# Query transposes moved to the DMA engines, with queries projected first, keys transposed in halves and token values kept in DRAM

## The chip, the cores and the metric

The kernel runs on one core of one Trainium2 chip. The metric is the device time of one execution in microseconds (us). The kernel before takes 1243.91 us in the median of the three runs that were at hand when the prediction was made (1236.84 to 1247.9). A time below is the median of all runs of a kernel, with their range. All runs quoted here gave the right result.

## The reference, cut to what matters

The work is one transformer block: a recurrent attention over 64 segments of 32 tokens with eight memory rows, then a gated feed-forward part.

```python
mem = mem0                                        # 8 rows of 640
for s in range(n_seg):                            # 64 segments, one after the other
    xs = x[:, s * seg_len:(s + 1) * seg_len, :]   # 32 tokens, layer-normed
    h = jnp.concatenate([mem, xs], axis=1)        # 40 rows
    q = jnp.einsum('btd,dhe->bhte', h, Wq)        # 32 heads of 128; k and v likewise
    scores = jnp.einsum('bhqe,bhke->bhqk', q, k) * scale
    p = softmax(where(mask, scores, -1e9))
    o = jnp.einsum('bhqk,bhke->bhqe', p, v)
    o = jnp.einsum('bhte,hed->btd', o, Wo)
    mem = o[:, :M, :]                             # the next segment's memory
    outs.append(o[:, M:, :])
...                                               # then h + FFN(layernorm(h))
```

The memory makes the loop a recurrence: the projections of segment s+1 can't begin before the memory rows of segment s have gone through the scores, the value product and the output projection. Whatever is late on that path is paid 62 times.

## The kernel before

Each segment projects a tile of 32 rows: the eight memory rows, and with them 24 token rows ("riders") of later segments. Four segments make a block. The 32 tokens of a block that find no place as riders ("extras") are projected separately, their keys at the end of a segment of position 2 (segment number mod 4), their queries in position 3, their values in position 0. Token keys wait in a ring `Kr`, token queries in `Qr`, token values in a ring `Vr`. `KS` holds the transposed keys of the current tile, `Vp` its values.

A projection leaves two [128, 512] tiles (four head groups of 32 rows each) in PSUM. They are copied to SBUF (`tok`) and have to be transposed before they can enter the scores. Keys are transposed by DMA (`dma_t`), queries by TensorE (`trans8`). In the loop all DMAs are issued from one queue, SyncE's, in program order; a DMA whose input isn't ready holds up all behind it (in the changed kernel 47 loads of values hold it for up to 6.4 us each). The segment's body:

```python
project(a, ks, 1, (0,), (P2,));  to_tok(P2, 0, "act")      # keys first
project(a, ks, 1, (1,), (P3,));  to_tok(P3, 1, "dve")
dma_t(KS..., tokp[0][:, :], ..., [("KS",)])                # one transpose, 128 x 1024
if fin: fin()                                              # extras' queries: trans8
pv_x(s - 1, BQ[0]);  norm_x(BQ[0]);  trans_ox(s - 1)       # token value product of s-1
project(a, ks, 0, (0, 1), (P0, P1))                        # queries
to_tok(P0, 2, "act");  to_tok(P1, 3, "dve")
project(a, ks, 2, (0,), BQ[:1])                            # values, first half
trans8(tok[2], ..., tok[3], ..., P3)                       # query transposes on TensorE
...                                                        # copies to Qr, Kr
project(a, ks, 2, (1,), (T0,))                             # values, second half
scores(s);  exp_mem();  exp_x()
v_riders(par, t0, nr)                                      # Vp -> Vr, 4 or 8 small DMAs
pv_mem(s);  trans_om(s);  wo_pass(...)                     # memory path
to_act(s + 1, B(T1), bank(T1)[:, 0:160])                   # new memory rows, on VectorE
store_attn(...)                                            # 4 DMAs
if evac: evac()                                            # extras' token tiles, Kr transpose
if woe: woe_sum(BQ[0]);  woe_store(s // 4 - 1)             # 8 DMAs, end of position 1
```

Token values go from the tile to the ring within SBUF:

```python
for g in range(4):
    a = 32 * g + M + done
    dma(Vr[q][32 * g + o:32 * g + o + m, :, :], Vp[par][a:a + m, :, :], ...)
```

The softmax here doesn't subtract the row's maximum and nothing guards it: scores larger than these inputs give would overflow.

Of the kernel before, what the change touches and what calls it, by code (L numbers as in the profile page):

```python
# [163 lines left out]
def build_kernel(nc, A_x, A_mem0, A_Wq, A_Wk, A_Wv, A_Wo, A_seg_len, B_W_gate, B_W_up, B_W_down, out):  # L164
# [21 lines left out]
    xn2_d = nc.dram_tensor("xn2_d", [128, DC, TB], BF16)  # L186
    attn_d = nc.dram_tensor("attn_d", [S, 4, DC * 32], BF16)
# [34 lines left out]
    mca = ar.alloc("mca", [128, SEG], BF16)  # L222
# [4 lines left out]
    KS = ar.alloc("KS", [128, H, SEG], BF16)  # L227
    Kr = [ar.alloc(f"Kr{i}", [128, H, SEG], BF16) for i in range(RING // SEG)]
    Qr = ar.alloc("Qr", [128, H, RING // SEG, M + SEG], BF16)
    Vr = [ar.alloc(f"Vr{i}", [128, 8, VW], BF16) for i in range(RING // SEG)]  # L230
# [50 lines left out]
    for g in range(4):  # L281
        add("pool", lambda p, g=g: p.affine_select(mca[32 * g:32 * g + 32, :], mca[32 * g:32 * g + 32, :], [[1, SEG]],
                                                   ALU.is_ge, 0.0, base=0, channel_multiplier=-1),
            r=[("mca",)], w=[("mca",)])
    add("dve", lambda v: v.memset(mbd[:], 0.0), w=[("mbd",)])
    for g in range(4):
        add("dve", lambda v, g=g: v.memset(mbd[32 * g:32 * g + 32, 0, 8 * g:8 * g + 8], BIG), r=[("mbd",)], w=[("mbd",)])
        add("dve", lambda v, g=g: v.memset(mbd[32 * g:32 * g + M, 1, 8 * g:8 * g + 8], BIG), r=[("mbd",)], w=[("mbd",)])

    add("dve", lambda v: v.memset(bank(P1), 0.0), w=[B(P1)])  # L290
# [5 lines left out]
    for i in range(RING // SEG):  # L296
        add("pool", lambda p, i=i: p.memset(ap(Vr[i], Dh, [[VW, 8], [1, 1]]), 1.0), w=[("Vr1", i)])
# [95 lines left out]
    def evac_k(src, skey, t0, n, lo, eng):  # L393
        for q, o, m, lo in pieces(t0, n, lo):
            copy_op(eng, Kr[q][:, :, o:o + m], src[:, :, lo:lo + m], [skey], [("Kr", q)])

    def evac_q(b, t0, n, lo, eng):
        for q, o, m, lo in pieces(t0, n, lo):
            copy_op(eng, Qr[:, :, q, M + o:M + o + m], slots(b, lo, lo + m), [B(b)], [("Qr", q)])
# [4 lines left out]
    def v_riders(par, t0, n):  # L404

        done = 0
        while done < n:
            t = t0 + done
            q, o = seg_slot(t // SEG), t % SEG
            m = min(n - done, SEG - o)  # L410
            for g in range(4):
                a = 32 * g + M + done
                dma(Vr[q][32 * g + o:32 * g + o + m, :, :], Vp[par][a:a + m, :, :], r=[("Vp", par), ("Vp1", par), ("Vr1", q)],
                    w=[("Vr", q, g, o)])
            done += m

    def vr_keys(q):
        return [("Vr", q)] + [("Vr1", q)] + [("Vr", q, g, o) for g in range(4) for o in (0, 8, 16, 24)]
# [11 lines left out]
    def ln1_back(b, src, r, eng):  # L430
# [13 lines left out]
        for j in range(full):  # L444
            copy(act_r[b % 2][:, j, :, M:32], src[:, :, RID * j:RID * (j + 1)], [("act", b % 2, "x", j)])
        if n == 128:
            copy(act_e[b % 2][:, :, :], src[:, :, 96:128], [("acte", b % 2)])
        elif n % RID:
            copy(act_r[b % 2][:, full, :, M:M + n % RID], src[:, :, RID * full:n], [("act", b % 2, "x", full)])
# [12 lines left out]
    def to_act(s, wkey, src):  # L462

        b, j = s // 4, s % 4
        add("dve", lambda v: v.transpose(TBf[:].rearrange("p c t -> p (c t)"), src), r=[wkey], w=[("TBf",)])  # L465
        add("dve", lambda v: v.tensor_copy(act_r[b % 2][:, j, :, 0:M], TBf[:, :, 0:M]), r=[("TBf",)],  # L466
            w=[("act", b % 2, j, "m")])
# [3 lines left out]
    def scores(s):  # L471

        q = seg_slot(s)

        def f(pe):
            for k in range(8):
                for a in range(2):
                    for g in range(4):
                        h = 4 * k + g
                        if a == 0:  # L480
                            o, lh = bank(P0)[32 * g:32 * g + 32, 40 * k:40 * k + 40], Kr[q][:, h, :]
                        else:
                            o, lh = bank(P1)[32 * g:32 * g + M, 40 * k:40 * k + 40], KS[:, h, 0:M]
                        i = pe.matmul(o, lh, Qr[:, h, q, :], start=True, stop=True, skip_group_check=True)  # L484
            return i
        add("pe", f, r=[("KS",), ("Qm", q), ("Kr", q), ("Qr", q)], w=[B(P0), B(P1)])

# [13 lines left out]
    def exp_x():  # L501
        add("act", lambda a: a.activation(Px[:, :].rearrange("p (a k q) -> p a k q", a=2, k=8), s_view(M, M + SEG),
                                          ACTF.Exp, scale=SCALE), r=[B(P0), B(P1)], w=[("Px",)])
        add("dve", lambda v: v.tensor_tensor(ap(Px, 0, [[32, 8], [1, 32]]), ap(Px, 0, [[32, 8], [1, 32]]),
                                             ap(mca, 0, [[0, 8], [1, 32]]), ALU.min), r=[("Px",), ("mca",)],
            w=[("Px",)])

    def pv_mem(s):
        q = seg_slot(s)
        par = s % 2  # L510
        for a in range(2):
            def f(pe, a=a):
                t = Vr[q] if a == 0 else Vp[par]
# [6 lines left out]
            add("pe", f, r=[("Pbd", a)] + ([("Vp", par), ("Vp1", par)] if a else vr_keys(q)), w=[B(T1)])  # L520
# [5 lines left out]
    def trans_om(s):  # L526
# [5 lines left out]
        copy_op("dve", ap(oT[s % 2], 0, [[16 * SEG, 2], [SEG, 4], [4 * SEG, 4], [1, M]]),  # L532
# [29 lines left out]
    def store_attn(src, skey, p0, t0, n):  # L562
        for g in range(4):
            dma(attn_d[t0:t0 + n, g, :], src[32 * g + p0:32 * g + p0 + n, :, :].rearrange("p c j -> p (c j)"),
                r=[skey], w=[("attn", t0, g)])

    def pv_x(s, b0):
        q = seg_slot(s)
        par = s % 2

        def f(pe):
            for kh in range(2):
                for a in range(2):
                    for c in range(4):
                        k = 4 * kh + c
                        for g in range(4):
                            n, t = (32, Vr[q]) if a == 0 else (M, Vp[par])
                            i = pe.matmul(bank(b0 + g)[32 * c:32 * c + 32, 129 * kh:129 * kh + 129],  # L578
                                          Px[32 * g:32 * g + n, 256 * a + 32 * k:256 * a + 32 * k + 32],
                                          t[32 * g:32 * g + n, k, 0:129], start=(a == 0), stop=(a == 1),  # L580
                                          skip_group_check=True, tile_position=(32 * g, 32 * c))
            return i
        add("pe", f, r=[("Px",), ("Vp", par), ("Vp1", par)] + vr_keys(q), w=[B(b0 + g) for g in range(4)])
# [15 lines left out]
    def copy_oTe(s):  # L599
        o = M * (s % 4)  # L600
        copy_op("dve", oTe[:, :, o:o + M], oT[s % 2][:, :, 0:M], [("oT", s % 2, "m")], [("oTe", s % 4)])


    def attn_keys(i):
        ks = []
        for s in range(4 * i, 4 * i + 4):
            ks += [("attn", 32 * s + M, g) for g in range(4)] + [("attn", 32 * s, g) for g in range(2)]
        return ks
# [29 lines left out]
    for g in range(4):  # L638
        dma(wtok[1][32 * g:32 * g + M, :, :],
# [27 lines left out]
    def opening_back(j, n, bk):  # L667
        t = 2 * (n % 2)
        trans8(tok[t], ("tok", t), tok[t + 1], ("tok", t + 1), bk)
        if n > 0:  # L670
            eng = ("dve", "act")[n - 1]
            if j == 1:
                evac_k(slots(bk, 0, SEG), B(bk), 32 * (n - 1), 32, 0, eng)
            else:
                evac_q(bk, 32 * (n - 1), 32, 0, eng)
            return
        q = seg_slot(0)
        if j == 1:
            copy_op("dve", KS[:, :, 0:M], slots(bk, 0, M), [B(bk)], [("KS",)])
            evac_k(slots(bk, 0, SEG), B(bk), 64, RID, M, "act")  # L680
        else:
            copy_op("dve", Qr[:, :, q, 0:M], slots(bk, 0, M), [B(bk)], [("Qm", q)])
            evac_q(bk, 64, RID, M, "act")
# [19 lines left out]
    for i in range(2):  # L703
        for n, (a, ks) in enumerate(groups):
            q = seg_slot(n - 1)
            t, key = (Vr[q], ("Vr", q)) if n else (Vp[0], ("Vp", 0))
            project(a, ks, 2, (i,), vbanks[n][i:i + 1])
            to_v(vbanks[n][i], t, i, key, ("act", "dve")[(i + n) % 2])
    v_riders(0, 64, RID)
# [15 lines left out]
    def extra_units(s):  # L725
# [15 lines left out]
        def evac():  # L741
            for i, e in enumerate(("act", "dve")):
                if j == 2:
                    to_v(BQ[i], Vr[q], i, ("Vr", q), e)
                else:
                    to_tok(BQ[i], 2 + i, e)
            if j == 1:
                dma_t(Kr[q][:].rearrange("p h t -> p (h t)").rearrange("p (k r) -> p k r", r=128), tokp[1][:, :],
                      [("tok", 2), ("tok", 3)], [("Kr", q)])

        def fin():
            trans8(tok[2], ("tok", 2), tok[3], ("tok", 3), P2)
            evac_q(P2, t0, 32, 0, "act")
        return part, evac, (fin if j == 0 else None)
# [10 lines left out]
    def woe_store(b):  # L765
        for j in range(4):
            for dg in range(2):
                t0 = 32 * (4 * b + j)
                dma(attn_d[t0:t0 + M, 2 * dg:2 * dg + 2, :].rearrange("t g f -> t (g f)"),
                    ap(Pbd, 0, [[1, 320]], 32 * dg + M * j, M), r=[("Pbd", 0), ("Pbd", 1)], w=[("attn", t0, dg)])  # L770

    fin = None
    for s in range(NSEG):
# [13 lines left out]
        if s > 0:  # L787
            a, ks = pass_act(s)
            t0, nr = rider_tokens(s)
            project(a, ks, 1, (0,), (P2,))  # L790
            to_tok(P2, 0, "act")
            project(a, ks, 1, (1,), (P3,))
            to_tok(P3, 1, "dve")
            dma_t(KS[:].rearrange("p h t -> p (h t)").rearrange("p (k r) -> p k r", r=128), tokp[0][:, :],
                  [("tok", 0), ("tok", 1)], [("KS",)])
            if fin:
                fin()
            pv_x(s - 1, BQ[0])
            norm_x(BQ[0])
            trans_ox(s - 1)  # L800
            n = n_rows(nb) if s % 4 == 2 and ln else 128 if e2b is not None else 0
            if n:
                row_scale(xt, ("xt",), n, xt, ("xt",))
                dma_t(chunks_of(at[:, :])[:, :, 0:n], xt[0:n, :], [("xt",)], [("at",)])
# [6 lines left out]
            project(a, ks, 2, (0,), BQ[:1])  # L811
            to_v(BQ[0], Vp[par], 0, ("Vp", par), "act")
            if not last:
                trans8(tok[2], ("tok", 2), tok[3], ("tok", 3), P3)
# [226 lines left out]
```

## Time and profile before

| | before |
|---|---|
| time | 1243.91 us (1236.84 to 1247.9, 3 runs) |
| span of the profiled run, granted TensorE clock | 1245.2 us, 0.983 |
| opening / 62 segments / feed-forward tail | 62.2 / 971.7 / 211.3 us |
| segment mean, positions 0 / 1 / 2 / 3 | 15.65 / 14.83 / 16.48 / 15.60 us |
| half-clock time within the loop | 24.4 us, 7 stretches |

The rows from the third on are my sums over the trace. Position 2 is given without the next-to-last segment of the loop, which also loads weights (with it 16.61). A segment runs from the VectorE transpose of one segment's memory rows (`TBf`) to the next one's.

From the page of the kernel before: busy time, the clock in tenths over 40 slices, and the engines' shares of the chain of work that ended last. A group's columns are: line, engine and operation, output and inputs, count, then busy us and mean ns, then the idle time ahead of it and what ended most of it.

```profile
PE 1114.9 (90%) x30140; PEld 577.0 (46%) x27792; DVE 564.4 (45%) x1438; ACT 333.2 (27%) x684; POOL 25.3 (2%) x92
...
PEclk9889999999999999999999999999999998999999
...
PE 77%; DMA 11%; DVE 6%; SPq 3%; issue 3%; ACT 1%; DVEq 0%
...
L350 PE MATMUL ps<-W,act_r 128*32 128x512 bf16 x6640 | 456.5, 385 | 27.7 <-DVE act_r L466 12.7
...
L369 PE MATMUL ps<-ident,tok 128*128 128x128 bf16 x664 | 51.2, 220 | 17.9 <-DVE tok L378 13.3
...
L484 PE MATMUL ps<-Qr,Kr 128*32 128x40 bf16 x2048 | 41.9, 186 | 25.2 <-DMA KS<-tok 25.0
```

TensorE sets the time: it is busy for 90% of the span and makes up 77% of the chain. The query transposes (L369) cost it 51.2 us and 17.9 us of waiting. The scores (L484) wait 25.0 us in all for the transposed keys.

Four successive segments, that one first (window, its length, then busy us of PE, PEld, DVE, ACT and POOL with counts, granted clock, DMA share, GB/s):

```profile
657.75:674.34 16.59, 14.05 (x450) 7.40 (x402) 7.05 (x19) 4.16 (x8) 0.00 (x0) 1.00 0.53 87
674.34:690.44 16.10, 14.38 (x458) 7.59 (x410) 8.92 (x24) 5.57 (x11) 0.00 (x0) 1.00 0.40 86
690.44:705.80 15.36, 14.00 (x466) 8.20 (x442) 7.20 (x19) 4.22 (x9) 0.00 (x0) 1.00 0.28 55
705.80:721.24 15.44, 14.14 (x456) 7.20 (x407) 8.33 (x23) 4.66 (x11) 1.48 (x5) 1.00 0.36 68
```

TensorE is busy for 14.0 to 14.4 us of each, at full clock.

### The profile page before, as it was taken

What the parts mean: (1) busy time and instruction counts of PE and PEld (TensorE: products, weight loads), DVE (VectorE), ACT (ScalarE), POOL (GpSimd) and SP (SyncE); (2) the same over time, 40 slices, a digit from 0 to 9 for tenths busy, and PEclk for the clock granted to TensorE, in tenths of its full rate; (3) what the DMA queues carried; (4) which work ended last, traced back from release to release, by engine and by line L of the source; (5) the groups of instructions that cost most, each with busy time, mean ns of one, the idle gap of its engine ahead of it and who ended that gap; (6) DMA issues with size and microseconds to landing.
All of it is one profiled execution on the core that took longest, in us unless ns stands there. A gap on an engine that the chain in (4) does not pass through costs nothing.

```text
span 1245.2 us, 62156 instructions
## 1 busy us (share of the span) xinstructions
PE 1114.9 (90%) x30140; PEld 577.0 (46%) x27792; DVE 564.4 (45%) x1438; ACT 333.2 (27%) x684; POOL 25.3 (2%) x92
## 2 busy tenths in 40 slices
PE   5589999989899989989988989999989986999998
PEld 2344445444445544544444544454445454533443
DVE  3244545444444444554544544454445442443522
ACT  2123223322232222232322222233223321211311
POOL 1000000000000000000000000000000000000000
PEclk9889999999999999999999999999999998999999
DMA  9933333324343334343434344423242329121200
GB/s 360 337 53 68 58 67 59 66 57 67 56 66 59 70 57 66 60 81 66 79 70 81 66 82 64 65 55 79 42 78 57 63 58 323 27 80 27 69 22 22
DMA packets 218274, 102.12 MB, mean 82 GB/s; under 512 B 190688, under 2 KB 206752, under 8 KB 218016
## 3 DMA queue, kind: packets, MB, share of 16 engines
q1 hardware_dynamic: 217824, 98.13, 36.8%
q8 instruction: 227, 3.72, 1.3%
q14 instruction: 31, 0.25, 0.1%
q10 hardware_dynamic: 192, 0.01, 0.0%
HBM read 36.79 MB, written 6.55 MB: 35 GB/s over the span
## 4 chain that ended last, share of the span: by engine, by line
PE 77%; DMA 11%; DVE 6%; SPq 3%; issue 3%; ACT 1%; DVEq 0%
PE ps L350 27%; PE ps L541 13%; PE ps L336 10%; PE ps L883 10%; DMA KS<-tok 5%; DMA Kr<-tok 3%; SPq L306 3%; PE ps L484 3%; PE ps L369 3%; PE ps L916 3%; PE ps L578 3%; PE ps L553 2%; DMA Wo<-in_A_Wo_dram 2%; PE ps L517 2%; DVE TBf L465 2%
## 5 line engine op out<-in xcount | busy, mean ns | idle before, releaser
L350 PE MATMUL ps<-W,act_r 128*32 128x512 bf16 x6640 | 456.5, 385 | 27.7 <-DVE act_r L466 12.7
L350 PEld LDWEIGHTS ps<-W,act_r 128*32 128x32 bf16 x6640 | 170.0, 97 | 275.4 <-issue 74.3
L541 PE MATMUL ps<-Wo,oT 128*32 128x160 bf16 x8448 | 165.3, 236 | 35.2 <-DVE oT L378 23.8
L378 DVE CAST tok<-ps 128x512 bf16<-128x512 f32 x161 | 111.1, 690 | 151.6 <-PE ps L350 97.3
L541 PEld LDWEIGHTS ps<-Wo,oT 128*32 128x32 bf16 x8448 | 149.1, 98 | 49.5 <-DVE oT L378 35.5
L376 ACT ACTIVATE tok<-ps 128x512 bf16<-128x512 f32 x161 | 95.9, 596 | 249.9 <-PE ps L336 134.6
L336 PE MATMUL ps<-W,act_r 128*32 128x512 bf16 x1240 | 120.6, 379 | 0.3 <-issue 0.3
L376 ACT ACTIVATE wtok<-ps 128x160 bf16<-128x160 f32 x64 | 19.5, 304 | 311.4 <-DVE TBf L465 302.3
L465 DVE STREAM_TRANSPOSE TBf<-ps 128x160 f32<-128x160 f32 x64 | 22.4, 350 | 174.6 <-PE ps L541 174.6
L350 PE MATMUL ps<-W,act_e 128*32 128x512 bf16 x900 | 94.2, 395 | 1.5 <-issue 1.5
L336 PE MATMUL ps<-W,act_e 128*32 128x512 bf16 x900 | 93.3, 392 | 0.8 <-issue 0.8
L591 DVE TENSOR_TENSOR ox<-ps,rx 128x512 bf16<-128x512 f32 x128 | 82.5, 686 | 2.2
L376 ACT ACTIVATE Qr<-ps 128x768 bf16<-128x768 bf16 (+3 forms) x110 | 69.2, 658 | 42.0 <-DVE Qr L378 26.7
L369 PE MATMUL ps<-ident,tok 128*128 128x128 bf16 x664 | 51.2, 220 | 17.9 <-DVE tok L378 13.3
L883 PE MATMUL ps<-xn2T,Wg 128*128 128x512 bf16 x260 | 65.6, 383 | 0.0
L883 PE MATMUL ps<-xn2T,Wu 128*128 128x512 bf16 x260 | 65.5, 383 | 0.0
L484 PE MATMUL ps<-Qr,Kr 128*32 128x40 bf16 x2048 | 41.9, 186 | 25.2 <-DMA KS<-tok 25.0
L898 DVE TENSOR_TENSOR hT<-g,ps 128x512 bf16<-128x512 bf16 (+1 forms) x56 | 38.5, 688 | 57.1 <-PE ps L883 53.3
L916 PE MATMUL ps<-Wd,hT 128*128 128x320 bf16 (+1 forms) x240 | 63.3, 300 | 0.0
L369 PEld LDWEIGHTS ps<-ident,tok 128*128 128x128 bf16 x664 | 37.4, 98 | 52.8 <-DVE tok L378 48.0
L378 DVE CAST Vp<-ps 128x512 bf16<-128x512 f32 x64 | 44.1, 689 | 33.1 <-PE ps L350 33.1
L896 ACT ACTIVATE g<-ps 128x512 bf16<-128x512 f32 (+1 forms) x56 | 32.5, 593 | 95.9 <-PE ps L883 95.9
(82 smaller groups left out, 1006.1 us busy)
## 6 DMA issues: line engine op xcount, KB each, us to landing
Vr<-Vp SPq DMA_DIRECT2D x124, 48.8 KB
W<-in_A_Wk_dram SPq DMA_DIRECT2D x2, 2560.0 KB
W<-in_A_Wq_dram SPq DMA_DIRECT2D x2, 2560.0 KB
W<-in_A_Wv_dram SPq DMA_DIRECT2D x2, 2560.0 KB
Wo<-in_A_Wo_dram SPq DMA_DIRECT2D x2, 2560.0 KB
xt<-in_A_x_dram SPq DMA_DIRECT2D x30, 160.0 KB
Vr<-Vp SPq DMA_DIRECT2D x128, 32.5 KB
attn_d<-wtok SPq DMA_DIRECT2D x256, 7.5 KB
```

What stands on the lines that cost most here:

```text
L336: return pe.add_instruction(mybir.InstMatmult(name=nc.get_next_instruction_name(), engine=mybir.EngineType.PE, ins=[pe.lower_ap(rhs), pe.l ...
L350: ins = pe.matmul(*a, start=(c == 0), stop=(c == DC - 1), skip_group_check=True)
L369: ins = pe.matmul(bank_bf(b)[:, k * 128:(k + 1) * 128], t[:, (k % 4) * 128:(k % 4 + 1) * 128], ident[:, :], is_transpose=True)
L376: add("act", lambda a: a.activation(dst, src, ACTF.Copy), r=r, w=w)
L378: add("dve", lambda v: v.tensor_copy(dst, src), r=r, w=w)
L465: add("dve", lambda v: v.transpose(TBf[:].rearrange("p c t -> p (c t)"), src), r=[wkey], w=[("TBf",)])
L484: i = pe.matmul(o, lh, Qr[:, h, q, :], start=True, stop=True, skip_group_check=True)
L541: i = pe.matmul(bank(bk)[32 * gg:32 * gg + 32, 0:160], src[:, hb, :], w[:, gg], start=(hb == 0), stop=(hb == 31), skip_group_check=True)
L591: add("dve", lambda v, kh=kh: v.tensor_tensor(ox[:, kh, :, :], src[:, :, kh, 0:128], ap(rx, kh, [[2, 4], [0, 128]]), ALU.mult), r=[B(b0 + ...
L883: ins = pe.matmul(bank(bk), w[:, c, lo:lo + 128], xn2T[par][:, c, :], start=(c == 0), stop=(c == DC - 1))
L898: add("dve", lambda v: v.tensor_tensor(hT[par][lo:128, j, :], g1[gi][lo:128, :], bank(bu)[lo:128, :], ALU.mult), r=[B(bu), ("g1", gi)], w= ...
L916: i = pe.matmul(*a, start=(j == 0), stop=(j == FC - 1), skip_group_check=True)
```

## The change

The intent: take the query transposes off TensorE (about 43 us of its time) and cut SyncE's 8 to 16 issues per segment to about 7.

1. Queries are projected first and transposed by DMA into a new tile `QS`.
2. Keys come second, each half transposed by its own DMA as soon as it is there.
3. Then the token value product of the segment before, and values last, both halves at once.
4. Token values go through DRAM (`v_d`): the whole tile is stored in one DMA, and a segment's 32 rows are loaded in one DMA. So are the attention rows (4 DMAs become 1) and the memory's output rows (8 become 2).
5. The extras' queries wait in DRAM (`q_d`) and are transposed on reload; the extras use the token tiles of the keys.

The core of the diff (cuts marked):

```diff
-    def v_riders(par, t0, n):
-        ...                                  # 4 or 8 DMAs within SBUF
+    def v_rows(t0):
+        return bass.AP(v_d, t0 * 8 * VW, [[(S + 32) * 8 * VW, 4], [8 * VW, 32], [1, 8 * VW]])
+
+    def v_store(par, t0):
+        dma(v_rows(t0), Vp[par][:].rearrange("p k d -> p (k d)"), r=[("Vp", par), ...], w=[("v_d",)])
+
+    def v_load(s):
+        dma(Vr[s % 2][:].rearrange("p k d -> p (k d)"), v_rows(SEG * s), r=[("v_d",)], w=[("Vr", s % 2)])
...
+        dma(bass.AP(attn_d, SEG * s * D, [[160, 4], [D, SEG], [1, 160]]), src[:]..., w=[("attn", s)])
...
+                project(a, ks, 0, (0, 1), (P0, P1))
+                if s == NSEG - 2:
+                    load_gate_up()
+                to_tok(P0, 2, "act")
+                to_tok(P1, 3, "dve")
+                dma_t(runs(QS), tokp[1][:, :], [("tok", 2), ("tok", 3)], [("QS",)])
+            for i in range(2):
+                project(a, ks, 1, (i,), ((P2, P3)[i],))
+                to_tok((P2, P3)[i], i, ("dve", "act")[i])
+                dma_t(runs(KS)[:, 4 * i:4 * i + 4, :], tok[i], [("tok", i)], [("KS", i)])
+            pv_x(s - 1, T0)
+            norm_x(T0)
+            trans_ox(s - 1)
+            if not last:
+                copy_op("dve", Qr[:, :, q, 0:M], QS[:, :, RID:32], [("QS",)], [("Qm", q)])
+            project(a, ks, 2, (0, 1), BQ)
...                                           # scores in two halves, exponentials, row scaling
+            if nr:
+                v_store(par, t0)
+                evac_q(QS, ("QS",), t0, nr, 0, "act")
+        eq = fin
+        if eq:
+            dma_t(runs(QS), q_d[:, :], [("q_d",)], [("QS",)])
...                                           # memory path up to to_act(s + 1, ...)
+        if s > 0 and (s + 1) % 4 != 1:
+            v_load(s + 1)
         if s >= 2:
             wo_rows(T1, wtok[par], ("wtok", par), "act")
+            store_attn(wtok[par], ("wtok", par), s - 2)
```

## The prediction

> **What bounds the kernel now.** TensorE is busy 1114.9 of 1245.2 us (page, part 1). The change plays in 62 recurrent segments (timeline); opening (62 us) and feed-forward tail (about 210 us) hardly see it. By position in a block of four, segment means are 15.7, 14.7, 16.6 and 15.6 us; the undisturbed minimum is 14.4. The rest is waiting and throttled clock:
> - scores waiting for the transposed keys: 25 us in 16 waits (view of waits), nearly all in position 2, where eight small stores and up to eight value copies stand ahead of the key transpose in SyncE's queue (issued at +5 to +9 us, not +3.7);
> - query transposes on TensorE waiting for token tiles: about 15 us, two thirds of it tiles that the ring-key transpose still reads;
> - five half-clock stretches of 3.4 us in the loop, about 1.5 us each, after waits of about 2 us. [...]
>
> **Removed.** Eight query transposes on TensorE per segment (0.55 us of its stream), eight more (0.6 us) in position 0: about 43 us, all on the path. SyncE issues drop from 8 to 16 per segment to about 7, so most of the 40 us of waits should go, and two or three clock drops.
>
> **Added.** One full transpose per segment, and the key transpose in two. A full one takes 1.27 us to issue and lands after 3.07 us at best, 3.6 in the median, over 4 when a 16 KB instruction fetch falls in. The 640-column ones issue in 1.20 and land after 2.56, so I estimate a half (512 columns) at 1.18 and 2.4: halving hardly shortens the issue. [...]
>
> Estimated new segment: queries end 2.9, query transpose issued 3.74; key halves issued 5.06 (lands 7.45) and 6.29 (lands 8.7). TensorE has queries, keys, x value product, values and half of the scores done at 8.07. So the second half of the scores waits at least 0.6 us everywhere, with fetches about 1.0. This disputed term eats what the removed transposes give, and decides the sign.
>
> Also: the mask on 512 instead of 256 columns (297 to about 430 ns, nearly hidden); row scaling now ahead of the memory normalisation, 0.4 us in position 2; in position 3 the first key half waits for the ring-key transpose (lands at about 5.1 to 5.7), 0.9 us; four early-block segments where VectorE may block on the late query reload, 1.5 us each. Values through DRAM (two 260 KB passes of about 2 us) have slack.
>
> **Sum.** Position 0 about -0.6 us per segment, 1: +0.3, 2: -1.2, 3: +0.4; times 15 or 16, about -16; opening and tail -2, early blocks +6: -12 us. If keys land early, -40.
>
> **Prediction: 1230 us, 8 in 10 between 1198 and 1258. Faster by over 2%: 0.40; within 2%: 0.51; slower: 0.09.**
>
> **Right if** TensorE's matmul time falls by about 40 us; position 2 falls from 16.6 to about 15.4 us; scores wait for keys in nearly every segment (0.6 to 1.3 us; 40 to 80 us in total), longest in position 3; half-clock stretches are no more than now.
>
> **Wrong if** half transposes issue in well under 1.2 us or land before 8.1 us (then 1185 to 1205); if three transposes in a row delay instruction fetches, or two-microsecond waits trip the clock in every position 3 (slower); if the value reload lands late and holds up SyncE's queue.

The 2 us for a pass of values was an estimate of mine; no trace then at hand held a transfer of that form.

## More of the kernel before

SyncE's queue in a segment of position 3 that begins at 657.75 (start, then length, in us; each line is one or more issues):

```profile
658.55 1.68 SPq L306 DMA_DIRECT2D attn_d<-wtok  x4
660.33 1.82 SPq L309 DMA_TRANSPOSE Kr<-tok  x1
662.19 0.59 SPq L306 DMA_DIRECT2D xt<-in_A_x_dram  x1
662.82 0.42 SPq L306 DMA_DIRECT2D at<-attn_d  x1
663.34 1.24 SPq L309 DMA_TRANSPOSE KS<-tok  x1
664.63 1.38 SPq L309 DMA_TRANSPOSE oT<-ox  x1
669.39 3.07 SPq L306 DMA_DIRECT2D Vr<-Vp  x4
```

Stores of the segment before stand ahead of the key transpose; even so it goes out 5.6 us into the segment and there is no long gap ahead of it.

## The result and the profile after

The changed kernel takes 1513.92 us (1510.35 to 1523.27, 4 runs); the kernel before took 1245.14 us (1236.84 to 1247.9, 4 runs) beside it. The ratio is 1.218, with a 95% interval of 1.210 to 1.227: over a fifth slower. A ratio here is the mean time of one kernel's fast runs over that of the other's fast runs in the same rounds, so it is not quite the ratio of the medians. Executions over 1.5% slower than the fastest of the same kernel are left out of the means.

| | before | after |
|---|---|---|
| span of the profiled run, granted clock | 1245.2 us, 0.983 | 1514.9 us, 0.893 |
| opening / 62 segments / tail | 62.2 / 971.7 / 211.3 | 61.8 / 1242.8 / 210.3 |
| segment mean, positions 0 / 1 / 2 / 3 | 15.65 / 14.83 / 16.48 / 15.60 | 17.69 / 18.04 / 21.07 / 22.63 |
| TensorE idle within the loop | 89.6 | 327.6 |
| of it ahead of the scores | 22.6 | 257.8 |
| half-clock time within the loop | 24.4, 7 stretches | 304.1, 48 stretches |

(Position 2 again without the next-to-last segment; with it 21.84.) All of the growth is in the loop: 271 us. TensorE's idle time grew by 238 us of it. The other 33 us are TensorE time. The removed transposes had taken 47.9 us in the loop, so the other matmuls took about 81 us more. Half clock can account for that. In half-clock stretches the trace records a granted clock of 0.50, and successive groups of four 128x512 matmuls of the projections (`act_r`) start 414 ns apart instead of 206 (medians, changed kernel). Within the loop TensorE was busy for 204.9 us in such stretches (22.9 before), and if half of that is stretching, the growth is about 91 us (my estimate).

From the page of the changed kernel:

```profile
PE 1148.4 (76%) x29524; PEld 543.3 (36%) x25916; DVE 563.5 (37%) x1452; ACT 312.9 (21%) x669; POOL 26.6 (2%) x99
...
PEclk9889889899979998989788998888988989799999
...
PE 49%; DMA 32%; SPq 10%; DVE 7%; issue 2%; ACT 1%; DVEq 0%
...
L355 PE MATMUL ps<-W,act_r 128*32 128x512 bf16 x5380 | 429.7, 391 | 28.1 <-DVE act_r L468 14.8
L341 PE MATMUL ps<-W,act_r 128*32 128x512 bf16 x2500 | 254.0, 389 | 1.4 <-issue 1.4
...
L483 PE MATMUL ps<-Qr,Kr 128*32 128x40 bf16 x2048 | 50.6, 193 | 258.7 <-DMA KS<-tok 255.0
```

The same matmuls of the scores now wait 255.0 us for the key transposes, where they waited 25.0. DMA and SyncE's queue went from 14% of the chain to 42%. The view of waits (us in all, times, longest) says how long each wait is and, with the last two lines, what SyncE's queue itself waits for:

```profile
PE ps L483 <- DMA KS<-tok: 255.0, 110, 17.0
ACT tok L381 <- DMA Kr<-tok: 106.8, 15, 8.7
DVE tok L383 <- DMA Kr<-tok: 105.6, 15, 8.7
SPq L311 <- DMA v_d<-Vp: 271.5, 47, 6.4
SPq L121 <- DMA attn_d<-wtok: 80.4, 16, 5.4
```

The fourth line is the key. There are 47 loads of values from DRAM, each waits at the head of SyncE's queue for the store of values before it, and they wait 271.5 us, up to 6.4 us each. The fifth line is the same fault in small. The attention rows are now stored with all 32 rows of a segment, the eight memory rows among them, and the memory's output rows are written over these later; so the store of the memory rows has to wait until the attention rows have landed. In the kernel before, the two wrote different rows. In each of the 15 segments of position 2 from segment 6 on, this holds SyncE's queue for 5.1 to 5.4 us. SyncE's queue through one segment of position 3, which begins at 567.90, and into the next, which begins at 591.30:

```profile
570.71 0.53 SPq L311 DMA_DIRECT2D Vr<-v_d  x1
571.29 0.54 SPq L311 DMA_DIRECT2D attn_d<-wtok  x1
571.93 2.23 SPq L314 DMA_TRANSPOSE Kr<-tok  x1
574.26 2.44 SPq L314 DMA_TRANSPOSE QS<-tok  x1
580.19 2.50 SPq L314 DMA_TRANSPOSE KS<-tok  x2
582.74 1.31 SPq L314 DMA_TRANSPOSE oT<-ox  x1
584.14 0.52 SPq L311 DMA_DIRECT2D v_d<-Vp  x1
590.56 0.55 SPq L311 DMA_DIRECT2D Vr<-v_d  x1
591.99 0.52 SPq L311 DMA_DIRECT2D attn_d<-wtok  x1
```

Read it with the landings, which I took from the semaphore increments in the trace. The value load stands at the head of the queue until 570.71, 2.8 us into the segment. Behind it come the attention rows and the transpose of the extras' keys (`Kr`), which lands only at 579.35, 7.4 us after its issue; in the kernel before this one landed 3.07 to 5.05 us after its issue. Keys can't be copied to their token tile before then, because the extras now use that tile, so the key halves go out at 580.19, land at 582.61 and 583.91, and TensorE, which would have reached the scores at about 576, has waited. The value store then goes out at 584.14 and lands at 590.54: 6.4 us for 260 KB. The next load leaves 0.02 us after that, and the next segment begins late too. The four segments from this one on:

```profile
567.90:591.30 23.40, 15.58 (x442) 7.25 (x374) 6.95 (x20) 3.97 (x8) 0.00 (x0) 0.85 0.54 80
591.30:610.50 19.20, 15.66 (x442) 7.13 (x374) 6.82 (x18) 4.08 (x8) 0.00 (x0) 0.82 0.74 106
610.50:625.80 15.30, 13.29 (x458) 7.16 (x414) 7.52 (x19) 4.17 (x9) 0.00 (x0) 1.00 0.49 78
625.80:648.20 22.40, 15.73 (x446) 7.20 (x382) 8.43 (x23) 4.62 (x11) 1.47 (x5) 0.85 0.38 69
```

The third is undisturbed and shows what was hoped for: 15.30 us with TensorE busy 13.29 us, about 0.7 us less than in the segment of the same position before (14.00). The others lose 3 to 8 us to waits, and then their clock drops to 0.82 to 0.85, which stretches TensorE's own time to 15.58 to 15.73 us.

**Why a 260 KB pass takes 6 us.** Its access pattern in DRAM is `[4][32][1040]`: the outermost dimension, the head group, has size 4. In both traces the number of semaphore increments that a DMA posts goes with that size. Of the copies of values in the kernel before (`Vr<-Vp`), those of 8 rows show 9 increments (124 of 124), those of 24 rows 13 (123 of 124) and those of 16 rows 16 (128 of 128). In the changed kernel each value store, value load and attention-row store shows 5 (one record of a store lacks one): in a load the first comes 0.97 us after the issue in the median, the other four only after 4.93 us or more. The transposes show 16 (all but one record of 313). The stored query tile, pattern `[128][1024]`, is nearly as large (256 KB), goes to DRAM too, and shows 16. The packets say the same: a pass moves as 128 of 2080 bytes, of which 3.6 (store) and 3.8 (load) are under way at a time in the mean (medians over the passes), never more than 8; the query tile moves as 128 of 2048 bytes, with 13 to 16 under way at the peak. I read this as four engines at work on a pass, of the 16 that the page counts; the trace does not name the engine of a packet. Below, "narrow" is a pass of this form, "wide" one cut so that each DMA has 32 rows outermost. I had not looked at the pattern when I predicted.

### The profile page after: what moved, and what is told of

It reads as the page before. It is cut to its first block, busy times and chain, and to the rows that moved or that the text cites. A ratio compares the mean times of both kernels' runs of the same rounds, so it can differ in the third digit from the quotient of the medians.

```text
span 1514.9 us, 59076 instructions
## 1 busy us (share of the span) xinstructions
PE 1148.4 (76%) x29524; PEld 543.3 (36%) x25916; DVE 563.5 (37%) x1452; ACT 312.9 (21%) x669; POOL 26.6 (2%) x99
## 4 chain that ended last, share of the span: by engine, by line
PE 49%; DMA 32%; SPq 10%; DVE 7%; issue 2%; ACT 1%; DVEq 0%
PE ps L355 13%; DMA KS<-tok 10%; PE ps L341 10%; PE ps L540 9%; PE ps L875 7%; DMA Kr<-tok 7%; SPq L314 6%; SPq L311 4%; DMA v_d<-Vp 4%; DMA attn_d<-wtok 3%; DMA q_d<-tok 3%; DMA QS<-q_d 3%; PE ps L908 2%; DMA Wo<-in_A_Wo_dram 2%; DVE tok L383 2%
## 5 line engine op out<-in xcount | busy, mean ns | idle before, releaser
L355 PE MATMUL ps<-W,act_r 128*32 128x512 bf16 x5380 | 429.7, 391 | 28.1 <-DVE act_r L468 14.8
L355 PEld LDWEIGHTS ps<-W,act_r 128*32 128x32 bf16 x5380 | 151.4, 99 | 305.2 <-issue 165.5
L341 PE MATMUL ps<-W,act_r 128*32 128x512 bf16 x2500 | 254.0, 389 | 1.4 <-issue 1.4
L483 PE MATMUL ps<-Qr,Kr 128*32 128x40 bf16 x2048 | 50.6, 193 | 258.7 <-DMA KS<-tok 255.0
L540 PEld LDWEIGHTS ps<-Wo,oT 128*32 128x32 bf16 x8448 | 154.2, 100 | 51.3 <-DVE oT L383 36.2
L483 PEld LDWEIGHTS ps<-Qr,Kr 128*32 128x32 bf16 x2048 | 37.5, 100 | 309.6 <-DVE Qr L383 123.9
L355 PE MATMUL ps<-W,act_e 128*32 128x512 bf16 x900 | 121.6, 526 | 0.0
L341 PE MATMUL ps<-W,act_e 128*32 128x512 bf16 x900 | 121.1, 524 | 0.0
L496 DVE TENSOR_TENSOR Pbd<-om,mbd 128x256 bf16<-128x256 bf16 x126 | 31.1, 289 | 116.6 <-ACT om L493 116.6
L383 DVE COPY Qr<-QS 128x256 bf16<-128x256 bf16 (+1 forms) x77 | 20.1, 261 | 137.2 <-DMA QS<-tok 98.8
L493 ACT ACTIVATE om<-ps 128x128 bf16<-128x128 f32 x63 | 17.4, 277 | 229.4 <-PE ps L483 229.4
L381 ACT ACTIVATE Vp<-ps 128x512 bf16<-128x512 f32 x64 | 38.1, 596 | 117.7 <-PE ps L341 117.5
```

The lines of the kernel that those rows point to most:

```text
L341: return pe.add_instruction(mybir.InstMatmult(name=nc.get_next_instruction_name(), engine=mybir.EngineType.PE, ins=[pe.lower_ap(rhs), pe.l ...
L355: ins = pe.matmul(*a, start=(c == 0), stop=(c == DC - 1), skip_group_check=True)
L381: add("act", lambda a: a.activation(dst, src, ACTF.Copy), r=r, w=w)
L383: add("dve", lambda v: v.tensor_copy(dst, src), r=r, w=w)
L483: i = pe.matmul(o, (Kr[q], KS)[a][:, h, :], Qr[:, h, q, :], start=True, stop=True, skip_group_check=True)
L540: i = pe.matmul(bank(bk)[32 * gg:32 * gg + 32, 0:160], src[:, hb, :], w[:, gg], start=(hb == 0), stop=(hb == 31), skip_group_check=True)
```

## The experiments

Theory A: the narrow passes (four engines, by the reading above) are the main cause. Theory B: the order in SyncE's queue is (the load behind the store, with all else behind it). Theory C: moving queries first and keys later, with transposes by DMA, is (my own disputed term, under-estimated). Each could make the scores wait for keys. The edits are against the changed kernel unless another is named; the time of the kernel before is the median of the same batch on the same chip. The batches ran on different chips, and the kernel before took 1238.7 to 1245.1 us in them, so a difference of a few us between runs of two batches says little.

### 1. Values in four DMAs, one per head group (spread_v), and attention rows likewise (spread_all)

```diff
-    def v_rows(t0):
-        return bass.AP(v_d, t0 * 8 * VW, [[(S + 32) * 8 * VW, 4], [8 * VW, 32], [1, 8 * VW]])
+    def v_rows(t0, g):
+        return bass.AP(v_d, (g * (S + 32) + t0) * 8 * VW, [[8 * VW, 32], [1, 8 * VW]])
+        for g in range(4):                   # store; the load likewise
+            dma(v_rows(t0, g), Vp[par][32 * g:32 * g + 32]..., w=[("v_d", g)])
+# spread_all also:
+        for g in range(4):
+            dma(bass.AP(attn_d, SEG * s * D + 160 * g, [[D, SEG], [1, 160]]), src[32 * g:32 * g + 32]..., ...)
```

The bytes and their place in DRAM stay the same; only the outermost dimension of each DMA is now 32.

> The change, but each of its three one-shot passes (value store to DRAM, value load from DRAM, attention rows to DRAM) is cut into four transfers of 32 partitions, same bytes, same places in the order. Theory A (the passes' outermost DRAM dimension is 4, so they run on 4 of 16 DMA engines, land after about 6 us, and hold up the in-order SyncE queue and the transposes behind them): each piece posts 16 increments and lands in 2.0 to 2.8 us, the scores' wait for keys falls from 258 us to 40 to 90 us, total 1200 to 1290 us. Rival B (the round trip through DRAM and the wait of the load for the store are slow in themselves): total stays above 1400 us. Rival C (three transposes in a row on the DMA engines are the cost, as my prediction feared): total above 1350 us, landings of the passes no longer long but the scores still wait over 150 us.

> As the former, but only the two value passes are cut in four; the attention rows still leave in one transfer on 4 engines. Theory A: most of the loss is the two 260 KB passes (5.8 and 6.4 us), the attention rows are small (40 KB, 2.2 us when nothing is ahead), so within 30 us of the former. If the attention rows matter by themselves (queue position just ahead of the transposes): 50 us or more slower than the former.

Measured: spread_all 1385.83 us (1379.92 to 1392.33), ratio 1.121 [1.115, 1.127] to 1238.72 of the kernel before; spread_v 1338.51 (1336.33 to 1350.0), ratio 1.086 [1.079, 1.092]. All pieces show 16 increments. From the transfer view of spread_v (the last column is the median us from issue to landing, which that view leaves empty for the narrow passes of the changed kernel), and its waits:

```profile
v_d<-Vp SPq DMA_DIRECT2D x252, 65.0 KB, 2.7
Vr<-v_d SPq DMA_DIRECT2D x188, 65.0 KB, 2.8
...
q_d<-tok SPq DMA_DIRECT2D x15, 256.0 KB, 2.3
...
PE ps L490 <- DMA KS<-tok: 129.3, 102, 16.6
SPq L121 <- DMA attn_d<-wtok: 29.0, 16, 2.4
SPq L311 <- DMA v_d<-Vp: 21.1, 48, 0.9
```

With wide passes the loads hold SyncE's queue for 21.1 us instead of 271.5, and the wait for the attention rows falls from 80.4 to 29.0. Counted from the increments: the store of the changed kernel landed 5.90 us after its issue at best and 6.40 in the median, the load 5.34 and 5.77. A piece of spread_v lands in 1.70 us at best, and the four pieces of a pass from the first issue to the last landing in 3.2 at best and 4.2 to 4.3 in the median. In the same run the query tile, one DMA of 256 KB with 16 increments, took 2.17 us in the median. So what makes a pass slow is neither DRAM nor its bytes but its width. Three more DMA issues per pass buy 175 us (1513.9 to 1338.5). The ring-key transpose behind them changes as well: 5.80 to 7.66 us in the changed kernel, against 3.05 to 4.32 in a wide kernel with mended order (experiment 4). That a transpose, with its 16 increments, has a share on the four loaded engines too is my reading; no trace shows it directly. The attention rows (40 KB, also 5 increments) landed 2.24 us after their issue at best, 5.72 in the median, mostly right behind the value load.

The expectations missed in two ways. Both kernels were to fall to 1200 to 1290 us, and the wait for keys to 40 to 90 us: the direction was right, the size was not. And spread_all was to be as fast as spread_v or faster; it is 47 us slower, most of it in positions 2 and 3. Four issues for the attention rows stand in the queue just before the transposes and push the query transpose from 4.49 to 6.48 us into the segment in position 2 and from 5.43 to 6.70 in position 3 (medians). Nor did they shorten the wait for the attention rows' landing: it holds the queue for 29.3 us in spread_all and 29.0 in spread_v.

Theory A stands as the largest cause, but 100 us over the kernel before remain.

### 2. Query transposes back on TensorE (q_on_pe)

```diff
-                dma_t(runs(QS), tokp[1][:, :], [("tok", 2), ("tok", 3)], [("QS",)])
+                trans8(tok[2], ("tok", 2), tok[3], ("tok", 3), P2)     # after the x value product
+                copy_op("dve", Qr[:, :, q, 0:M], slots(P2, RID, SEG), [B(P2)], [("Qm", q)])
```

> The change with the segment's query transposes put back on TensorE (the block's extra queries still go through DRAM); the narrow passes stay. Theory A: the narrow passes alone make the loss, so it stays above 1430 us. Rival C (transposes by DMA make the loss): back to 1250 to 1320 us.

Measured: 1543.56 us (1541.22 to 1551.61), ratio 1.250 [1.244, 1.255]. So the query DMA alone does not explain the loss; taking it away costs 30 us more. The wait only moved:

```profile
PE ps L374 <- DVE tok L383: 130.3, 31, 7.4
```

The transposes on TensorE write a PSUM bank whose last contents are the keys, and those can't be copied out while the token tile is held by the late ring-key transpose or the late query store. Before the narrow passes are mended, this experiment can't weigh theory C.

### 3. Narrow value passes on ScalarE's queue (act_queue)

```diff
-        dma(v_rows(t0), Vp[par]..., w=[("v_d",)])
+        dma(v_rows(t0), Vp[par]..., w=[("v_d",)], eng="act")
-        if s > 0 and (s + 1) % 4 != 1:
-            v_load(s + 1)                     # moved behind evac(), with eng="act"
```

> The change with the two value passes still in one transfer each on 4 engines, but issued from ScalarE's queue, the load at the end of the segment, so that SyncE's order no longer makes the transposes wait for them. If theory A works through the in-order queue (a load that waits at the head for the store's landing): 1230 to 1330 us. If it works through the 4 loaded DMA engines, which the transposes share whatever the queue: above 1380 us.

Measured: 1433.14 us (1430.02 to 1443.59), ratio 1.161 [1.155, 1.167]. The passes are as narrow as ever, but no load holds up SyncE's queue. That gives 81 of the 270 us; wide passes in SyncE's queue gave 175. The time falls in the band that was named for the loaded engines (above 1380 us). So the blocked queue is a real part, but not all: with no load at its head, the ring-key transpose still landed only 6.01 to 7.49 us after its issue, against 3.16 to 5.02 in spread_v.

### 4. The order in SyncE's queue, mended, with wide and with narrow passes (wide_order, narrow_order)

```diff
             to_v(BQ[1], Vp[par], 1, ("Vp", par), "dve")
+            if nr:
+                v_store(par, t0)             # ahead of the scores
 ...
-            n = n_rows(nb) ...               # row scaling, its transpose, xn2_d store
+            evac_q(QS, ...);  dma_t(runs(QS), q_d[:, :], ...)   # now ahead of these
+            n = n_rows(nb) ...
 ...
-                if s == NSEG - 2:
-                    load_gate_up()           # was ahead of the query transpose
+            if s == NSEG - 2:
+                load_gate_up()               # now after trans_ox
```

> Value passes cut in four (as in spread_v, 1338 us) and three places in SyncE's order mended: the value store is issued as soon as the values are evicted, the block's query reload before the feed-forward transposes, and the gate and up weights after the last query and key transposes. Theory A2 (what is left after the width is the in-order queue: the load at its head waits for a store issued late): positions 2 and 3 lose 1 to 3 us each, segment 62 falls from 32.5 to about 17 us, total 1230 to 1290 us. If what is left is the transposes' own landing (rival C): above 1310 us, only segment 62 falls.

> The same mended order, but the passes stay one transfer each on 4 engines. If width and order are separate faults that add: about 80 to 100 us below the change, 1410 to 1440 us. If the order alone was the fault: below 1320 us. If the width is what matters and order only counts when it is right: above 1470 us.

Measured: wide_order 1294.63 us in the median of all four runs (1275.85 to 1297.4). Its two fast runs took 1275.85 and 1292.32, in the mean 1284, and its ratio, of these two, is 1.035 [1.027, 1.043]; it scatters more than the others, so differences to it are good to about 10 us. narrow_order took 1459.98 (1449.59 to 1465.9), ratio 1.176 [1.170, 1.182], which lies between the two bands that were named for it (1410 to 1440, above 1470). The order mends are worth about 54 us with wide passes (1338.5 to 1284) and 54 with narrow ones; width is worth about 176 us with mended order and 175 without. The two causes add. The order mends hold two smaller finds. In the next-to-last segment of the loop, the changed kernel issues the 4 MB of gate and up weights ahead of the last query transpose; this one wait of 17.0 us made that segment 33.4 us (18.6 before), and it is 17.9 in wide_order, though the later load costs the tail 8 us (210 to 218). And in four segments (33, 37, 41 and 45) TensorE stood still for 17.4 us in all in the changed kernel, because VectorE was held by the late reload of the extras' queries; that wait is gone.

wide_order is still 44 us slower than the kernel before (fast runs), and little of that looks due to values: their loads hold the queue for 23.9 us. Its scores wait 113 us for keys, 108.5 of it within the loop:

```profile
PE ps L490 <- DMA KS<-tok: 112.9, 113, 8.5
```

### 5. What is left: queries on TensorE, ScalarE's queue, one key transpose (wide_order_qpe, wide_act, k_whole)

The edits are those of experiments 2 and 3 on wide_order; but wide_act also moves the value store back behind the exponentials, so it differs from wide_order in two things. For k_whole, on wide_order:

```diff
-                dma_t(runs(KS)[:, 4 * i:4 * i + 4, :], tok[i], [("tok", i)], [("KS", i)])
+            dma_t(runs(KS), tokp[0][:, :], [("tok", 0), ("tok", 1)], [("KS", 0), ("KS", 1)])
```

> wide_order with the segment's query transposes on TensorE again: what the query transposes by DMA are worth with the passes mended. If they pay as intended: 20 to 45 us slower than wide_order. If my prediction's term was right (what they give is lost again as a wait for keys): within 10 us of it. If they harm (rival C): faster by over 20 us.

> wide_order with the eight pieces of the value passes issued from ScalarE, so that SyncE's queue holds only transposes and rows. If SyncE's issue time (0.4 to 0.5 us a piece) and its order still matter: 10 to 50 us faster than wide_order, and key transposes issued at their earliest (+5.1 and +6.3 us) in positions 0 to 2. If only the traffic on the engines matters: the same as wide_order within 10 us.

> wide_order (1294 us) with the keys transposed in one transfer after both halves are evicted instead of two halves. A whole one issued at about +5.8 us lands at 8.9 at best, the second half at 8.7: if halving hardly shortens the issue, as I predicted, the total stays within 15 us of wide_order; if the halves matter as intended, it is over 25 us slower.

Measured: wide_order_qpe 1262.75 us (1260.01 to 1263.72), ratio 1.017 [1.015, 1.020]; wide_act 1303.45 (1303.12 to 1305.21), ratio 1.051 [1.049, 1.053]; k_whole 1277.81 (1273.8 to 1287.58), ratio 1.031 [1.023, 1.038].

With wide passes, query transposes on TensorE are about 21 us *faster* than by DMA in the same order (fast runs; the intervals of the ratios do not overlap). I had expected them to be 20 to 45 us slower; this is theory C's side of the record. The wait for keys falls to less than half, since the key transposes no longer stand behind the query transpose:

```profile
PE ps L490 <- DMA KS<-tok: 47.3, 67, 8.1
```

wide_act is about 19 us slower than wide_order, where I had expected a gain or no change; since its store is also later, this does not weigh ScalarE's queue alone. Keys in halves bring nothing: the whole transpose is about 6 us faster by the fast runs, and the intervals of the ratios overlap. A half transpose takes 1.19 us to issue at best and 1.28 in the median (wide_order), a whole one 1.23 and 1.27 (k_whole).

### 6. Width again, the other way: two halves (halves)

```diff
+        return bass.AP(v_d, (2 * g * (S + 32) + t0) * 8 * VW, [[(S + 32) * 8 * VW, 2], [8 * VW, 32], [1, 8 * VW]])
+        for g in range(2):                   # store and load as two DMAs of 130 KB
```

> The change with each value pass cut in two transfers of 64 partitions, whose outermost DRAM dimension is 2. Theory A (the number of engines follows the outermost dimension): [...] lands later than the single transfer did (over 9 us instead of 5.8 to 6.4), and the kernel is slower than the change, over 1600 us. Rival B2 (a transfer of 260 KB is long because it is large, and cutting it is what helped): lands in 3 to 5 us and the kernel lies between the change and spread_v, 1380 to 1470 us.

Measured: 1655.19 us (1652.43 and 1657.94), ratio 1.333 [1.322, 1.345]. Like spread_v this cuts a pass into more DMAs, but the outermost dimension is now 2. Each DMA shows three increments, the number that theory A had named. The first half of a pass lands 5.4 us after its issue at best and 5.6 to 5.9 in the median, about what the uncut pass took. That would be 32 rows for each engine in both cases, if three increments stand for two engines as five do for four (my reading). The pair takes 8.65 us (load) and 9.15 us (store) in the median, less than two in a row but much more than one, which would fit halves that share engines; the trace does not show which they use. I had expected each half to be over 9 us; that held for the pair only. The scores' wait follows:

```profile
PE ps L490 <- DMA KS<-tok: 358.6, 112, 19.0
```

So it was not the number of DMAs that made spread_v fast.

### 7. Keys first again, with the wide passes (keys_first), the same with narrow ones (narrow_keys_first), and the kernel before with its queue mended (before_mend)

keys_first takes from the change the passes through DRAM, cut in four, and the merged row stores, and puts the segment's body back: keys first in one transpose, the token value product, queries, first values, query transposes on TensorE, second values, then the value store. The extras use the token tiles of the queries again. narrow_keys_first is the same with the uncut passes.

```diff
+            for i in range(2):                         # keys
+                project(a, ks, 1, (i,), ((P2, P3)[i],))
+                to_tok((P2, P3)[i], i, ("act", "dve")[i])
+            dma_t(runs(KS), tokp[0][:, :], [("tok", 0), ("tok", 1)], [("KS", 0), ("KS", 1)])
+            pv_x(s - 1, BQ[0]);  norm_x(BQ[0]);  trans_ox(s - 1)
+            ...                                        # queries, values 0, trans8 to P3, values 1
+            if nr:
+                v_store(par, t0)
```

before_mend, against the kernel before: the eight stores of the memory's output rows become two, and the attention rows leave after the ring-key transpose.

```diff
-                dma(attn_d[t0:t0 + M, 2 * dg:2 * dg + 2, :]..., ap(Pbd, 0, [[1, 320]], 32 * dg + M * j, M), ...)   # x 8
+            dma(bass.AP(attn_d, 128 * b * D + 320 * dg, [[SEG * D, 4], [D, M], [1, 320]]), ...)                    # x 2
-            store_attn(wtok[par], ("wtok", par), M, 32 * (s - 2) + M, RID)   # ahead of evac()
+            store_attn(wtok[par], ("wtok", par), M, 32 * (s - 2) + M, RID)   # behind it
```

> The order of before (keys first, in one transpose, then x value product, queries, values; query transposes on TensorE), with the riders-first layout and the mended value passes and merged row stores of the change. If queries first and keys late is what makes the scores wait (my prediction's term): the wait for keys falls below 15 us in the loop and the total is 1190 to 1235 us. If the value passes through DRAM cost even when wide: no faster than 1250 us.

> keys_first (1214 us) with the value passes as single transfers on 4 engines again: the fourth corner of width against order of the projections (narrow and queries first 1460, wide and queries first 1295, wide and keys first 1214). If the narrow passes cost the same everywhere, because they hold SyncE and four engines for 12 us of each segment whatever else is done: 1360 to 1400 us. If they harm mainly because queries first leaves the keys no slack: 1240 to 1320 us. If the order alone was the fault: within 2% of keys_first.

> The kernel before with two places of its SyncE queue mended: the eight small stores of memory rows merged in two (outermost dimension 4, small: about 2 us), and the ring-key transpose ahead of the attention rows. The waits for keys in position 2 (about 20 us) and of the query transposes in position 3 (about 10 us) should shrink by half or more, with two or three clock drops: 1205 to 1230 us.

Measured: keys_first 1214.21 us (1212.08 to 1220.0), ratio 0.979 [0.973, 0.985] to 1242.37; before_mend 1223.08 (1219.92 to 1224.38), ratio 0.985 [0.978, 0.991]; narrow_keys_first 1392.57 (1380.07 to 1398.6), ratio 1.119 [1.111, 1.128] to 1241.03. All three fell within their bands. The record's verdict at 2% is "unclear" for keys_first and for before_mend, since their intervals reach across 0.98; both lie clear of 1. keys_first from its page and its view of waits:

```profile
PE 1097.7 (91%) x30005; PEld 569.0 (47%) x27672; DVE 574.2 (47%) x1452; ACT 318.0 (26%) x669; POOL 27.3 (2%) x99
...
PE 73%; DMA 10%; DVE 8%; SPq 5%; issue 3%; ACT 1%; DVEq 0%
...
PE ps L490 <- DMA KS<-tok: 5.1, 7, 3.3
SPq L311 <- DMA v_d<-Vp: 9.0, 11, 5.6
```

With keys first, the scores wait 5.1 us for them in the whole run. The order of the segment, with the transposes that go with it, is worth about 70 us with wide passes (1284 to 1214.2) and 67 with narrow ones. Width is worth 178 us even here, where scores hardly depend on the order. And keys_first beats both kernels of this case; the interval puts it 1.5 to 2.7% below the kernel before. Much of that may not be owed to DRAM: before_mend, with one store merged and one moved, gains 1.5%, and the two intervals overlap. The gains differ in place, though: before_mend's is all in position 2 (16.61 to 15.04 us a segment), keys_first's in position 2 (to 15.27) and in position 0 (15.65 to 14.56), where the extras' queries are no longer transposed on TensorE.

### Eight runs side by side

Spans of the loop, TensorE's idle time in it ahead of the scores, and half-clock time in it, all in us, from the traces:

| run | loop | idle at scores | half clock |
|---|---|---|---|
| before | 971.7 | 22.6 | 24.4 |
| after | 1242.8 | 257.8 | 304.1 |
| spread_v | 1064.3 | 141.5 | 114.6 |
| wide_order | 1010.6 | 108.5 | 65.1 |
| wide_order_qpe | 980.1 | 42.0 | 14.1 |
| keys_first | 934.2 | 1.9 | 5.3 |
| before_mend | 948.6 | 15.4 | 13.9 |
| halves | 1376.5 | 356.3 | 444.7 |

Half-clock time follows the waits down and up. In the loops half rate (granted clock 0.50 in the traces) comes in stretches of 3.41 us or whole multiples of it (in the kernel before six of one window and one of three, which began in the opening; in the changed one most of two). TensorE need not be idle for all of a window. I cut the loops of all 15 traces into such windows, in step with the changes of clock. At full clock, every window with more than 2.04 us without a matmul was followed by half clock, and none with less than 1.67; at half clock, full clock came back only after windows with at most 0.86, and after every one with less than 0.76. So in these runs waits of about 2 us that fell into one window were enough to drop the clock. No run separated the clock's share from the waits that bring it, so it is counted here as their consequence.

## Why the prediction was wrong, and where it was right

The prediction said 1230 us, 1198 to 1258; it took 1514.

**The step that failed** is the sentence "Values through DRAM (two 260 KB passes of about 2 us) have slack." A pass took 5.3 us at best and 5.8 to 6.4 in the median, because its access pattern, with 4 outermost, keeps only 3.6 to 3.8 packets under way at a time. At that length the load isn't ready when its turn comes; and since it stands at the head of the one queue, it holds up every transpose behind it: 271.5 us of waits in SyncE's queue where I had counted none. The passes cost 175 to 178 us by themselves, in each of three orders of the rest (1514 to 1339, 1460 to 1284, 1393 to 1214). Two microseconds would have been right for a pass of 128 rows outermost: the query tile took 2.17 in spread_v. My estimate went by the size; I did not check the shape. The last words of the prediction, "if the value reload lands late and holds up SyncE's queue", name the mechanism; I had it as a risk and gave the slower side 0.09.

**"SyncE issues drop from 8 to 16 per segment to about 7, so most of the 40 us of waits should go."** The issues did drop, from 14.9 to 8.8 a segment in the mean. The waits grew all the same, since an issue in the queue costs as long as it waits, not one unit. Position 2 was to fall from 16.6 to about 15.4 us and rose to 21.8 (21.1 without the next-to-last segment); there the merged store of memory rows waits besides for the attention rows to land, 80.4 us in 16 waits, which the prediction did not have.

**"Four early-block segments where VectorE may block ... 1.5 us each."** They blocked, and TensorE with them, for 4.1 to 4.5 us each, 17.4 in all.

**The load of gate and up weights** ahead of the last query transpose (17.0 us in one segment) was not seen at all.

**The disputed term** was right in kind and too small. "The second half of the scores waits at least 0.6 us everywhere, with fetches about 1.0": in wide_order, with the values' fault removed, scores wait 108.5 us in 62 segments, 1.75 us each. By experiment 5 and 7, late keys and query transposes in front of them outweigh the removed TensorE transposes. Even with the passes and the order mended, the intended form (wide_order, 1284 us by its fast runs, ratio 1.035) is slower than the kernel before, so the sign of the forecast would have been wrong also without the narrow passes. Its attention-row wait (29.0 us of SyncE's queue) was left in.

**Right:** TensorE reaches the scores about 8.1 us into a segment (predicted 8.07), half transposes issue in 1.19 us at best (1.27 in the median) and land after 2.40 at best, 2.50 in the median (predicted 1.18 and 2.4), and halving them hardly shortens the issue. A transpose's landing shrinks less than its columns: half of them, 2.40 us at best instead of 3.07. The about 43 us of TensorE time did go (the transposes had taken 47.9 us in the loop): wide_order's TensorE is busy 1087.6 us, 27 less than before at a lower granted clock (0.966 against 0.983), and the undisturbed segment above shows 13.29 us. In the changed kernel itself that is hidden: PE's busy time *rose* to 1148.4, by half-clock stretching (the estimate above).

What stays open: how the remaining 44 us of wide_order divide between the later key transposes and the query transposes ahead of them, beyond the 21 us that moving the latter to TensorE gives back; what the wait for attention rows costs, since no run removed it; and how much the dropped clock adds on its own.

## What to carry to other kernels

Before costing a DMA by its bytes, look at the outermost dimension of its patterns. Here one DMA of 260 KB with 4 outermost took 5.8 to 6.4 us in the median, four with 32 outermost 4.2 to 4.3 together, and one of 256 KB with 128 outermost 2.17. The trace shows this by the count of semaphore increments (5 against 16) and by transfers behind it that grow slow (the ring-key transpose, 5.80 to 7.66 us against 3.05 to 4.32). In a queue that issues in order, place a transfer by the moment its input is ready, and put nothing that waits ahead of what the critical path needs (271.5 us in 47 waits here); when stores are merged, look whether they now overlap others, since then one must wait for the other to land (5.1 to 5.4 us in each of 15 segments here). A transpose that feeds the critical path should be issued first and by itself; freeing the busiest engine gained nothing here, since its inputs then arrived later than it could use them (wide_order: TensorE busy 27 us less, the scores waiting 108.5 us for keys in the loop, the kernel 44 us slower).

## Further measurements

- A narrow pass, by row: from 32 rows of 2080 bytes per engine (5.34 to 5.90 us at best, changed kernel) to 2 rows (1.70, a piece of spread_v), about 0.12 to 0.14 us per row and engine. This is an estimate; it takes the pass to run on four engines and a piece on 16. The packets' records agree with it: one of 2080 bytes took 0.115 us (load) and 0.131 us (store) in the mean of a pass (median over the passes of the changed kernel).
- A small transpose between SBUF tiles, at best: 128 x 1024 in bf16 1.23 us to issue and 3.07 to land (kernel before); 128 x 512, 1.19 and 2.40 (changed kernel).
- Transposes and fetches of instructions: the trace records 227 fetches of 16 KiB in the kernel before. There the 16 key transposes with no such fetch between issue and landing landed in 3.25 us in the median (3.22 to 3.64), the 47 with one in 3.88 (3.07 to 5.04; 20 of them over 4). No run changed the fetches, so that they are the cause is not shown.
